# Two-head state blocks, paired w loads, u by matmul and a new instruction order in a fused linear-attention and mixing kernel

## Chip, cores, metric

One core of a Trainium2 chip. The metric is the device time of one execution in microseconds (us). "Span" is the profile's time from the first to the last instruction of one execution, some 1.7 us shorter. Ratios below are the mean time of one kernel's fast runs over that of the kernel before's fast runs of the same rounds, with a 95% interval, so not quite the ratio of the medians. A run counts as slow when it is over 1.5% above the fastest of its kernel; slow runs are left out of every ratio.

## The reference

```python
# B, H, S, D = 4, 8, 768, 48; all float32
for t in range(S):                                    # one state of 48 x 48 per head
    cur = einsum('bhd,bhe->bhde', u * k[t], v[t])
    y[t] = einsum('bhd,bhde->bhe', r[t], state + cur)
    state = w[t][..., None] * state + einsum('bhd,bhe->bhde', k[t], v[t])
x = y as (B, S, H*D)                                  # d_model 384
theta = x @ w_theta
mix = w_tok_r @ (x * cos(theta)) + w_tok_i @ (x * sin(theta))
un = x + mix
out = un + relu(un @ w_ch)
```

## The kernel before

Tokens go in 24 chunks of 128 (6 for each of 4 batches). In a chunk the decays are summed as logarithms by matmuls with triangular masks, exponentials give `a`, and q = r·a, k' = k·a turn the recurrence into matmuls: masked scores (`p`), their product with v, and the state of the chunk before times q. Heads sit in pairs: two heads of 48 dimensions, each padded to 64, fill 128 partitions. `ORDER` is a searched list of all operations; each engine receives its own in that sequence, and a number after a slash picks another engine. A buffer takes a free slot of its pool when its first writer is issued; `bank` is a pool of six 2 KB PSUM banks.

```python
SLOTS = {"cum": 1, "bank": 6, ...}

ys = [Buf("bank", [L, NP, D], f32) for _ in range(2)]        # y: one bank for each head of a pair
...
# state times q: 8 matmuls on 64 rows
def f_ys():
    for j in range(NP):                                      # NP = 4 pairs
        for e in range(2):
            ro = e * DP                                      # DP = 64
            nc.tensor.matmul(get(ys[e])[:, j, :], lhsT=get(qkt)[ro:ro + DP, j, :],
                             rhs=get(prev)[ro:ro + DP, j, :], start=(j == 0), stop=False, ...)
...
m = Buf("bank", [L, NP, D], f32)
def f_M():                                                   # state update: 8 matmuls of 64 columns
    if c > 0:
        nc.tensor.matmul(mt, lhsT=ident, rhs=get(prev), start=True, stop=False, ...)
    for j in range(NP):
        for e in range(2):
            h = 2 * j + e
            nc.tensor.matmul(mt[e * DP:(e + 1) * DP, j, :], lhsT=get(kk)[:, h, :], rhs=get(vb)[:, h, :], ...)
def f_S():
    nc.vector.tensor_tensor(get(Sb), get(m), get(alt).to_broadcast([L, NP, D]), op=ALU.mult)
...
def f_x():                                                   # two instructions
    for e in range(2):
        nc.vector.tensor_tensor(xv[:, e], get(ys[e]), bv[:, e], op=ALU.add)
...
nc.sync.dma_start(out=get(bf), in_=src[b, :, c*L:(c+1)*L, :].rearrange("h t d -> t h d"))   # 1024 runs of 192 B
nc.sync.dma_start(out=u_bc, in_=u.partition_broadcast(L))                                   # u, 192 KB
```

Of the kernel before, what the change touches and what calls it, by code (L numbers as in the profile page):

```python
# [10 lines left out]
AF = mybir.ActivationFunctionType  # L11
ALU = mybir.AluOpType

ORDER = """
669 1 97 0 98 2 670 671 672/1 99 101/1 104/1 3 102/1 108 109 110 113 114 111 112 685 4 103 686 105 106 107 9 21 100
145 117 118 5 6 677 217 218 7 121 10 13 687 688 11 115 8 128/1 129/1 219 122 123 14 126/1 124 119 146 125 25 120 148
22 132 130 133 15 147 150 169 17 23 149/1 12 127 170 171 152/1 153 176 238 172 134 116 139 156 678 157/1 131 679 154
173/1 140 18 19 135/1 239 680/1 241 158 193 174 137 138 161/1 180 665 689 136/1 220/1 240 16 20 151 159 181 141 142
194 221 177/1 200/1 661 24 162/1 195 182 183 198 143 227 155 201/1 160 228/1 163 165 144 197/1 185/1 186/1 666 204 673
28 690 667 691 668 202 175 199 178 205 206 166 681 26 223 224 164 187 179 692/1 209/1 207 167 229 232/1 184 210/1 188  # L20
230 208 211 189 196 27 33 213 30 168 203 662/1 713 190 721 214 233/1 714 715 222 191 225 212 29 192/1 31 226 37 722
231 717 693 215 242 674/1 245 716 34 723 234 235 725 675 663 236 32 35 216 724 718 243 237/1 269 729 719 682/1 720 726
727 730 246 676/1 41 733 734 731 244 683 809 701 818 735 684/1 249 732 728 270 262 736 250 247 810 251 252 263 264 267
265 819 286 271 827 820 293 287 821 694 253 811 266/1 822 254 39 812 695 813 36 289 696/1 38 288 310 273 828 290 248
274 664 275 829 276 277 697 42 311 313 278 268 279 43 256 255 258 40 257 830 831/1 291 272 259 823 814 824 280 297 294
312 45 282 705 44 334 298/1 335 281 49 702 815 283 709 337 295 336 46 832 260 284 299 315 47 292 296 703 261/1 53 57
302 48 54 836 285/1 737 704/1 314 833 300 304 741 738 317 341 305 834 339 301 55 51 739 303 698/1 306 50 307 321 742
743 52 338/1 322/1 699 308 309/1 700 837 318 323 740 342 745 324 59 325 845 345 838 316 328 839 58 746 846 56 747 358
326 327 319 329 840 61 340 346 347 350/1 359 360 706/1 343 379 320 344 330 351/1 361 847 62 841 707 331 65 848 364 332
849 63 842 352 843 708 365 380 333 382 850 710/1 711 348 851/1 66 712 349 67 354 353 403 381 427 362/1 69 749 355 816  # L30
368 854 70 60 369 825 370 73 748 371/1 372/1 64 363 404 356 357 405 366 367 373 374 855 375 753 744 406 68 407 852/1
410 856 857 863 376 377 82 428 386 408/1 414 411 750 384/1 754 378/1 751 757 858/1 383/1 434 752 415 755 71 758 387
759 76 756 430 872 390 760 416 881 429 75 385 412 432 873 409 419 397 864 435/1 451 431/1 420 452 398 413 391 392
417/1 418/1 865 85 882 388 438 874 454 395/1 453 396/1 423 393 394 475 883 424 826 421 389 399 422 476 482 456 859 884
455 72 439/1 478 400 477 890 83 866 458/1 885 499 860 480 861 80 867 440 441/1 875 500 459/1 442/1 462 74 401 436 90
81 433 483/1 463 876 402/1 425 426/1 443 444 891 501 479 892 520 445 464 886 437 502 77 465/1 457 460 887/1 486 521
466/1 461 447 446 469 467/1 523 487 893 448 488 862 468/1 899 522 491/1 470 489 503 492/1 449 505 450/1 471 481 765
490 894 509 78 472 835 473 484 766 510 877 474 895 878 495 896/1 767 504 761 485 762 900 79 879 511 496 763 888/1
525/1 506 527 512/1 497 498/1 769 513/1 764 773 493 777 901 897/1 770 771 526 768 778 524 494 779 908 87 853 909 507
508 538 902 772 575 528/1 529 926 774 775 544 868 539 903/1 514 515 530 592 91 545 516 910 93 911 869/1 551 568 517  # L40
531 576 780 904 547 518 546 623 95 935 519/1 624 870/1 532/1 548/1 781 549/1 782 917 912/1 555 86 599 569 776 783 784
905/1 533 571 570 936 918 577 89 906/1 534 625 572 552/1 556 913 536/1 889 550 88 914/1 593 616 562 640 927 537/1 594
915/1 573/1 595 557 597 937 560/1 919 944 535 553 920 928 596/1 921 561/1 938 554 598 558 92 579 617 540 618 945 580
541 542 871 563 559 581 84 939/1 543/1 564 946 916 603 953 565 620 604/1 584 619 94 585 566 929 922 582 641 954 621
583 574 567 923 642 930/1 605 588 600 627 601 924 955 578 907 586 608/1 606 589 628 607 789 790 956 587 590 591/1 940
791 880 629 957 644 643 785 941 793 602 630 817 786 787 609/1 632/1 646/1 633/1 647 931 650 96 932/1 792 612 794 613
651 795 796 622 933/1 648 626 962 958 788 942 614 844 652 655/1 631 610 963 656/1 611 615/1 959/1 645 636 637 960/1
971 653 634 649 635 947 948/1 898 654 638 797 925 943 657 639 964 798 949 801 799 961 658 659 660/1 1011 805 802 803
804 800 1001 972 806 965 807 981 1002 808 1003 966/1 967 973 974 1012 1013 950 951 1004 982 991 975 1014 968 1005 992
1006/1 1007 1015 993 983 1016 976/1 977 1008/1 1009/1 934 984 1021 1010 969 1022 1023 970 985 978/1 952 994 979/1 995  # L50
1017 980 1024 1025 1018 986 987 988 1019 989 1020 996 990 997 1026 1027 998 999 1000 1028 1029 1030
# [63 lines left out]
def kernel(  # L115
# [13 lines left out]
    nc = tc.nc  # L129
# [11 lines left out]
    MERGE = False  # L141
    HHW = set()
# [4 lines left out]
             "xT": 9, "sc": 3, "wf": 3, "wn": 3, "un": 4, "uT": 3, "o": 8}  # L147
# [12 lines left out]
    u_bc = cpool.tile([L, H, D], f32, name="u_bc")  # L160
    hpi = cpool.tile([L, 1], f32, name="hpi")
# [9 lines left out]
            for n in ("lw", "q", "k")}  # L171

# [15 lines left out]
    nc.vector.memset(hpi, HALF_PI)  # L188
    for n_ in ("lw", "q", "k"):
        for t_ in pads[n_]:  # L190
            nc.vector.memset(t_[:, :, D:], 0.0)
    make_upper_triangular(nc, mask_exc[:, 0, :], val=1.0, diag=False)
# [73 lines left out]
    def attention(n):  # L266
# [17 lines left out]
        ys = [Buf("bank", [L, NP, D], f32) for _ in range(2)]  # L284
# [50 lines left out]
        P.op("cuml" if last else "cum", f"cum{n}", [("PE", f_cum)], [lw], [cum])  # L335
# [90 lines left out]
        def f_ys():  # L426
            for j in range(NP):
                for e in range(2):
                    ro = e * DP
                    nc.tensor.matmul(get(ys[e])[:, j, :], lhsT=get(qkt)[ro:ro + DP, j, :],  # L430
                                     rhs=get(prev)[ro:ro + DP, j, :],
                                     start=(j == 0), stop=False, skip_group_check=True)

        def f_pS():
            f_p()
            f_ys()
        if MERGE and prev:
            P.op("pS", f"p{n}", [("PE", f_pS)], [qkt] + pr_, ph + ys)
        else:
            P.op("p", f"p{n}", [("PE", f_p)], [qkt], ph)  # L440
# [14 lines left out]
        if not last:  # L455
            m = Buf("bank", [L, NP, D], f32)
            Sb = s["S"] = Buf("S", [L, NP, D], bf16)

            def f_M():
                mt = get(m)  # L460
                if c > 0:
                    nc.tensor.matmul(mt, lhsT=ident, rhs=get(prev), start=True, stop=False,  # L462
                                     skip_group_check=True)
                for j in range(NP):
                    for e in range(2):
                        h = 2 * j + e
                        nc.tensor.matmul(mt[e * DP:(e + 1) * DP, j, :], lhsT=get(kk)[:, h, :],  # L467
                                         rhs=get(vb)[:, h, :], start=(c == 0 and j == 0), stop=True,
                                         skip_group_check=True)
            P.op("M" if c > 0 else "M0", f"M{n}", [("PE", f_M)], [kk, vb] + ([prev] if prev else []), [m])  # L470

            def f_S():
                nc.vector.tensor_tensor(get(Sb), get(m), get(alt).to_broadcast([L, NP, D]), op=ALU.mult)
            P.op("S", f"S{n}", [("DVE", f_S)], [m, alt], [Sb])

        def f_y():
            if prev and not MERGE:
                f_ys()
            for e in range(2):
                for j in range(NP):  # L480
                    nc.tensor.matmul(get(ys[e])[:, j, :], lhsT=get(p)[:, e, j, :],  # L481
                                     rhs=get(vb)[:, 2 * j + e, :],
                                     start=(c == 0 and j == 0), stop=True, skip_group_check=True)
# [168 lines left out]
```

## Time and profile before

| | before |
|---|---|
| median (lowest to highest, 3 runs) | 172.62 us (171.29 to 172.9) |
| span of the profiled run, clock | 168.7 us, 0.996 |
| busy: TensorE, VectorE, ScalarE, GpSimd | 142.2, 137.8, 118.6, 116.3 us |
| DMA packets, MB | 105990, 29.98 |

No engine is full over the whole span; the limits change from stage to stage, so the prediction reads busy time by stage. The lines for that stand in it. A group's line gives busy us and the mean ns of one instruction; the chain's pieces are start, length, what.

### The profile page before, as it was taken

The numbers are of one execution on the slowest core, as the hardware profiler recorded it, in microseconds if no ns is written. First come the engines' busy times: TensorE is split into PE (matmuls) and PEld (weight loads), VectorE is DVE, ScalarE is ACT, GpSimd is POOL, SyncE is SP. The second block draws the span as 40 slices with busy tenths as digits, with TensorE's granted clock in tenths as the row PEclk, the third lists the DMA queues.
The fourth block names the chain that finished last, engine by engine and source line by source line (L and its number), as shares of the span: only waits on it lengthen the run. The fifth ranks groups of instructions, "written<-read, shape, count | busy, mean of one in ns | idle before, by whom it ended". The sixth has DMA issues, their size and how long they took to land. (4 is left out here: it accounts for less than half of the span.)

```text
span 168.7 us, 4451 instructions
## 1 busy us (share of the span) xinstructions
PE 142.2 (84%) x1688; PEld 93.5 (55%) x1688; DVE 137.8 (82%) x284; ACT 118.6 (70%) x224; POOL 116.3 (69%) x126
## 2 busy tenths in 40 slices
PE   0437789488869999999876999999889999999990
PEld 0324466464446766676544767556556766666660
DVE  2364479999999999989999998699999898753462
ACT  3454788989558799999873889899976588460240
POOL 3021588987925959796996999999998876800030
PEclk9999999999999999999999999999999999999998
DMA  5999999999989999898999898995335711100055
GB/s 142 278 206 254 205 184 236 286 299 193 247 231 229 241 195 269 162 216 174 205 198 193 177 232 176 233 186 137 79 93 155 222 47 49 61 36 4 0 187 190
DMA packets 105990, 29.98 MB, mean 178 GB/s; under 512 B 100464, under 2 KB 104432, under 8 KB 105968
## 3 DMA queue, kind: packets, MB, share of 16 engines
q1 hardware_dynamic: 105968, 29.70, 78.7%
q8 instruction: 13, 0.21, 0.5%
q14 instruction: 9, 0.07, 0.2%
HBM read 24.97 MB, written 4.72 MB: 176 GB/s over the span
## 5 line engine op out<-in xcount | busy, mean ns | idle before, releaser
L545 PE MATMUL bank<-z_all,wtokT 128*128 128x384 bf16 x288 | 53.6, 326 | 1.8 <-DVE z_all L531 1.7
L545 PEld LDWEIGHTS <-wtokT 128*128 128x128 bf16 x288 | 26.5, 98 | 17.7 <-issue 2.4
L399 POOL TENSOR_TENSOR bon<-v,rub 128x384 bf16<-128x384 bf16 x24 | 21.9, 914 | 8.0 <-ACT v L351 3.8
L357 POOL TENSOR_TENSOR ruk<-ru,ink 128x384 bf16<-128x384 f32 x16 | 17.9, 1126 | 7.8 <-DVE ru L357 7.5
L330 ACT ACTIVATE a<-cum 128x768 f32<-128x768 f32 x24 | 19.5, 812 | 4.6 <-PE cum L326 3.0
L531 DVE TENSOR_TENSOR z_all<-x_all,sc 128x768 bf16<-128x768 bf16 x24 | 21.1, 894 | 1.2 <-ACT sc L525 1.2
L357 POOL TENSOR_TENSOR ru<-inr,u_bc 128x384 f32<-128x384 f32 x18 | 21.0, 1170 | 0.2
L343 POOL TENSOR_TENSOR k<-ink,a 128x384 bf16<-128x384 f32 x16 | 17.2, 1075 | 5.0 <-ACT alt L333 3.4
L444 DVE TENSOR_TENSOR p<-bank,mask_exc 128x512 bf16<-128x512 f32 x29 | 19.5, 681 | 1.0 <-PE bank L421 0.8
L579 POOL TENSOR_TENSOR o<-o,un 128x384 f32<-128x384 f32 x10 | 10.4, 1044 | 13.3 <-ACT o L576 13.3
L343 POOL TENSOR_TENSOR q<-inr,a 128x384 bf16<-128x384 f32 x13 | 14.9, 1147 | 5.7 <-ACT alt L333 3.8
L450 POOL TENSOR_SCALAR_AFFINE_SELECT p<-p 128x512 bf16<-128x512 bf16 x19 | 14.8, 780 | 4.9 <-ACT p L447 4.9
L493 DVE TENSOR_TENSOR x_all<-bank,bon 128x192 bf16<-128x192 f32 x48 | 14.7, 349 | 3.8 <-PE bank L481 2.3
L551 DVE TENSOR_TENSOR un<-bank,x_all 128x384 bf16<-128x384 f32 x24 | 12.8, 549 | 5.6 <-PE bank L545 3.0
L226 ACT ACT_TABLE_LOAD x12 | 15.4, 1283 | 1.0 <-PEq L636 0.8
L517 PE MATMUL bank<-wth,xT 128*128 128x384 bf16 x72 | 15.2, 327 | 0.8 <-DVE xT L506 0.6
L447 ACT ACTIVATE p<-bank 128x512 bf16<-128x512 f32 x19 | 11.3, 596 | 5.5 <-PE bank L421 4.9
L322 PE MATMUL cum<-lw,mask_exc 128*128 128x384 bf16 x24 | 8.9, 372 | 7.3 <-ACT lw L318 5.4
L522 ACT ACTIVATE sc<-bank 128x384 bf16<-128x384 f32 x24 | 11.8, 495 | 4.7 <-PE bank L517 2.5
L568 PE MATMUL bank<-wch,uT 128*128 128x384 bf16 x72 | 15.0, 325 | 0.0
L318 ACT ACTIVATE lw<-inw 128x384 bf16<-128x384 f32 x24 | 12.4, 525 | 3.6 <-DMA inw<-in_w_dram 3.6
L560 ACT ACTIVATE uT<-bank 128x384 bf16<-128x384 bf16 x14 | 6.6, 489 | 10.9 <-PE bank L556 10.8
(64 smaller groups left out, 309.1 us busy)
## 6 DMA issues: line engine op xcount, KB each, us to landing
inw<-in_w_dram SPq DMA_DIRECT2D x24, 192.0 KB, 4.3
inr<-in_r_dram SPq DMA_DIRECT2D x24, 192.0 KB, 4.3
ink<-in_k_dram SPq DMA_DIRECT2D x24, 192.0 KB, 4.2
inv<-in_v_dram SPq DMA_DIRECT2D x24, 192.0 KB, 4.2
out_dram<-o SPq DMA_DIRECT2D x24, 192.0 KB, 2.3
wf<-in_moe_w_tok_i_dram SPq DMA_DIRECT2D x6, 384.0 KB, 4.3
wf<-in_moe_w_tok_r_dram SPq DMA_DIRECT2D x6, 384.0 KB, 4.7
wf<-in_moe_w_theta_dram SPq DMA_DIRECT2D x1, 576.0 KB, 6.8
```

The costliest lines, as they stand in the source:

```text
L226: nc.scalar.preload_act_table_set("trig_and_small" if mode == "S" else "natural_log_exp_and_others")
L330: nc.scalar.activation(get(a), get(cum)[:, :, :DM], AF.Exp)
L343: eng.tensor_tensor(get(o)[:, :, :D], get(x), av, op=ALU.mult)
L357: eng.tensor_tensor(o_, get(x), y if y is u_bc else get(y), op=ALU.mult)
L399: nc.gpsimd.tensor_tensor(get(bon), get(vb), get(rub).to_broadcast([L, H, D]), op=ALU.mult)
L444: nc.vector.tensor_tensor(get(p)[:, e], get(ph[e]), mask_exc.to_broadcast([L, NP, L]), op=ALU.mult)
L450: nc.gpsimd.affine_select(out=get(p)[:, e], in_=get(p)[:, e], compare_op=ALU.is_gt, fill=0.0, base=0, pattern=[[0, NP], [1, L]], channel_m ...
L493: nc.vector.tensor_tensor(xv[:, e], get(ys[e]), bv[:, e], op=ALU.add)
L517: nc.tensor.matmul(get(th), lhsT=get(s["xT"])[:, j, :], rhs=wth[:, j, :], start=(j == 0), stop=(j == NJ - 1))
L531: nc.vector.tensor_tensor(z_all[:, b, c], xb, get(sc), op=ALU.mult)
L545: nc.tensor.matmul(get(ac), lhsT=wtokT[:, q_, s_, ti, :], rhs=z_all[:, b, s_, q_, :], start=(s_ == 0 and q_ == 0), stop=(s_ == NCH - 1 and ...
L568: nc.tensor.matmul(get(ml), lhsT=get(uT)[:, j, :], rhs=wch[:, j, :], start=(j == 0), stop=(j == NJ - 1))
```

## The change

Intent: fewer and wider matmuls for the state (four of 128 rows and 96 columns in place of eight half-size ones), which takes a state padded with zeros off the diagonal of each pair; y then needs one bank instead of two; larger packets for w in chunks 1 to 8 (two neighbouring tokens are contiguous, 384 B); and no 192 KB broadcast of u. The order was searched anew.

```diff
-    HHW = set()
+    HHW = set(range(1,9))            # chunks whose w comes in token pairs (code already there:
+                                     # two loads of 64 partitions, 8+4 small matmuls for the sums)
-        ys = [Buf("bank", [L, NP, D], f32) for _ in range(2)]
+        ys = Buf("bank", [L, H, D], f32)
-            m = Buf("bank", [L, NP, D], f32)
+            m = Buf("bank", [L, NP, 2, D], f32)          # state tiles: zeroed once, [L, NP, 2, D]
                 for j in range(NP):
-                    for e in range(2):
-                        nc.tensor.matmul(mt[e*DP:(e+1)*DP, j, :], lhsT=get(kk)[:, h, :], rhs=get(vb)[:, h, :], ...)
+                    nc.tensor.matmul(mt[:, j], lhsT=get(kk)[:, 2*j:2*j+2, :], rhs=get(vb)[:, 2*j:2*j+2, :], ...)
             def f_S():
-                nc.vector.tensor_tensor(get(Sb), get(m), get(alt).to_broadcast([L, NP, D]), op=ALU.mult)
+                for e in range(2):
+                    rows = slice(e * DP, (e + 1) * DP)
+                    nc.vector.tensor_tensor(get(Sb)[rows, :, e, :], get(m)[rows, :, e, :],
+                                            get(alt)[rows].to_broadcast([DP, NP, D]), op=ALU.mult)
-            (state times q: eight matmuls on rows ro:ro+64)
+                for j in range(NP):
+                    nc.tensor.matmul(y[:, 2*j:2*j+2, :], lhsT=get(qkt)[:, j, :], rhs=get(prev)[:, j], ...)
-            for e in range(2):
-                nc.vector.tensor_tensor(xv[:, e], get(ys[e]), bv[:, e], op=ALU.add)
+            nc.vector.tensor_tensor(x_all[:, b, c, :]..., get(ys), get(bon), op=ALU.add)
-    u_bc <- u.partition_broadcast(L)                                 (DMA)
+    u_row <- u (1.5 KB DMA); u_ps = one_row.T @ u_row (TensorE); u_bc = copy of u_ps (ScalarE)
-ORDER = (old list)
+ORDER = (new list)
```

## The prediction

> **What bounds the kernel now.** I read the busy shares by slice first, then busy time by stage, then the chain that ended last, then the groups by shape. The slices, each 4.2 us wide:
>
> ```profile
> PE   0437789488869999999876999999889999999990
> DVE  2364479999999999989999998699999898753462
> DMA  5999999999989999898999898995335711100055
> ```
>
> The DMA engines are full from the start to about slice 27 (114 us), VectorE is full from slice 6 to 30, TensorE from slice 26 to the end. Three stages, three limits. Busy time by stage (columns: stretch and length, then busy us and instructions of PE, PEld, DVE, ACT, POOL, then clock, DMA share, GB/s):
>
> ```profile
> 0.00:24.00 24.00, 11.88 (x111) 8.22 (x112) 10.90 (x33) 12.84 (x24) 8.09 (x17) 1.00 1.04 216
> 24.00:100.00 76.00, 66.66 (x874) 44.28 (x872) 73.98 (x141) 62.20 (x117) 63.14 (x63) 1.00 1.03 220
> 100.00:150.00 50.00, 48.83 (x604) 32.00 (x603) 44.47 (x95) 39.91 (x76) 43.27 (x46) 1.00 0.53 129
> 150.00:168.70 18.70, 14.81 (x105) 8.98 (x103) 8.46 (x18) 3.69 (x8) 1.79 (x2) 0.96 0.24 86
> ```
>
> Until 24 us VectorE idles 13.1 us while DMA runs at a share of 1.04: loads set the pace. From 24 to 100 us VectorE is busy 74.0 of 76 us, with DMA still at 1.03. From 100 us on TensorE is busy 48.8 of 50. The DMA share of the small loads is a matter of packets, as the DMA view of 14 to 26 us shows:
>
> ```profile
> DMA packets 12768, 2.43 MB, mean 202 GB/s; under 512 B 12767, under 2 KB 12767, under 8 KB 12767
> q1 hardware_dynamic: 12767, 2.41, 106.9%
> ```
>
> 12 us x 16 engines x 1.069 / 12767 = 16.1 ns for a packet of 192 bytes, so 1024 of them (one 192 KB load) cost 1.0 us. The chain is, after 100 us, nearly all TensorE in queue order, and its pieces are start-to-start times (start, us, what):
>
> ```profile
> 102.46 0.33 PE bank L421 x8
> 102.79 1.08 PE bank L545 x6
> 103.87 0.17 PE bank L499 x3
> 104.04 0.20 PE bank L430 x8
> 104.24 0.31 PE bank L481 x8
> ...
> 136.49 0.08 PE bank L462
> 136.57 0.24 PE bank L467 x8
> 136.81 0.59 PE bank L517 x3
> ...
> 139.64 0.49 PE bank L568 x3
> ```
>
> Six 384-column matmuls take 0.97 us elsewhere in this chain and 1.08 after L421; three take 0.49 and, after L467, 0.59. So leaving a row- or column-tiled group (L421 scores, L430 state times q, L467 state update) costs some 0.10 us. The groups that I price with (busy us, mean ns):
>
> ```profile
> L473 DVE TENSOR_TENSOR S<-bank,alt 128x192 bf16<-128x192 f32 x20 | 6.9, 347 | 0.1
> L493 DVE TENSOR_TENSOR x_all<-bank,bon 128x192 bf16<-128x192 f32 x48 | 14.7, 349 | 3.8 <-PE bank L481 2.3 <-POOL bon L399 1.2
> L551 DVE TENSOR_TENSOR un<-bank,x_all 128x384 bf16<-128x384 f32 x24 | 12.8, 549 | 5.6 <-PE bank L545 3.0 <-POOL o L579 2.6
> ```
>
> **What the Trainium skill says.** (1) "TensorEngine Tiling (Array Packing)", Key Properties: changing the tiling mode drains TensorE. The trace agrees, with 0.10 us per change. (2) "TensorE: Matmul & The Clock Gate", under "Wait — 56ns, not 53.3ns?": starts never lie closer than about 25 ns. L430's eight 48-column matmuls take 0.20 us, 25 ns each, and not the 20 ns of their columns; four 96-column ones (estimate 40 ns each from 163 ns per 384) are therefore cheaper than eight. (3) "DMA: Bandwidth & Descriptors", Specifications: below 512 B a transfer is not at line rate. The 16.1 ns per 192 B above agree; what 384 B cost no run shows yet. (4) "SBUF — State Buffer", Who interferes with whom: a VectorE instruction with two SBUF inputs contends with a GpSimd one that reads SBUF. z (L531), same shape each time, lasts 541 to 1365 ns here, median 850.
>
> **The change part by part.**
>
> *State update.* Eight 48-column matmuls into two column tiles become four 96-column ones, and the identity matmul that carries the state goes from 192 to 384 columns. Before: 0.08 + 0.24 + 0.10 for leaving the mode = 0.42 us. After: 0.16 + 4 x 0.04 = 0.32. Gain 0.10 us.
>
> *State times q.* Before 0.20 + 0.30 (the L481 matmuls behind it, which take 0.22 where no tiled group precedes) = 0.50. After 0.16 + 0.22 = 0.38. Gain 0.12. Over about 20 chunks both make 4.4 us of TensorE, of which half (chunks 12 on) lies in the TensorE-bound part.
>
> *VectorE.* The state is now scaled by two instructions on 64 partitions instead of one on 128: the same length per partition, so +0.27 us start to start, 20 times, +5.4 us. The sum x becomes one 384-column instruction (0.46 start to start, as for un) in place of two (0.53): -1.7 us. The new order moves more: masking on VectorE 29 to 40 (+11 x 0.60), final relu+add 14 to 23 (+9 x 0.46), against q 11 to 3 (-8 x 0.83), copies of the transposed q,k 17 to 10 (-7 x 0.60), casts 6 to 2. Summing all instructions ahead of the last x by the mean durations gives 141.7 us before, 139.1 after: VectorE is not relieved by much. ScalarE goes from 119 to 121, GpSimd from 118 to 112 by the same sum. The mix is kinder to the shared port, since eight two-SBUF-input products leave VectorE.
>
> *w in token pairs, chunks 1 to 8.* 512 packets of 384 B instead of 1024 of 192 B; estimate 0.65 us for a load instead of 1.0, so -2.6 us of DMA over eight. The price is 12 small matmuls for the running sums instead of 6: estimate +0.1 us each on TensorE, in a stage where it has room, and 10 small GpSimd instructions at the start (2.7 us, hidden behind the first load).
>
> *u.* A 192 KB broadcast load becomes 1.5 KB, one matmul and one ScalarE copy (0.49 us): -0.6 us of DMA at the very start.
>
> *Order.* Reading the two orders against each other and pricing loads at 1.0 (small), 0.65 (paired) and 1.3 us (384 KB of weights), the load of v for chunk 11 ends its queue at 69.6 us before (it was issued at 67.8 to 69.5 us, so the sum is sound) and at 65.5 after: -4.1. k of chunk 4 stands behind 25.8 us of loads before, 12.0 after, as weights move back. So VectorE's 13.1 idle us at the start should shrink.
>
> **The sum**, in profile time, cut where z of chunk 11 ends (86.7 us) and where the last angle matmul (chunk 23) ends (150.4 us). *First part:* loads -4.1, VectorE idle perhaps -3, VectorE work about -1; the engines are in lockstep, so I credit 2.5. *Second part:* TensorE bound, 61.7 us of queue before and 58.3 after (y -1.2, state update -0.9 and one fewer of them, three final matmul groups deferred -1.5, one transposition more +0.5); 3.4 less, of which I credit 2.5, as VectorE is 89% busy there. *Last part:* 14.3 us of TensorE before (60 + 21 wide matmuls, 7 transposes), 15.2 after (60 + 27, 6): +0.9. Total -4.1 of 168.7, so 164.6; times 172.62/168.7 gives 168.4. I take **168.3 us**.
>
> **Rivals.**
>
> *A, VectorE takes it all back.* Scaling the state adds 5.4 us to the engine that is full from 24 to 100 us, and it sits on the recurrence from chunk to chunk. For it: 74.0 busy of 76. Against: the same order takes as much off VectorE elsewhere, and L473 idles it only 0.1 us. It would leave 171 to 173 us.
>
> *B, loads are hidden.* The waits show only 3.6 us of ScalarE and 2.3 us for inputs, so shorter loads would not matter after 24 us; then the first part gives 1 us or less and the time is 170. For it: VectorE full from 24 us. Against: the 13.1 us idle before that, and the early k loads.
>
> *C, more than I credit.* The sum x needs one bank instead of two of the six, so scores and transposes can start earlier, and the order was searched with that freedom. If the idle of the start falls by 4 us and TensorE's whole 3.4 us comes through, the time is 165 us.
>
> *D, the searched order does not carry over.* A tight order that depends on modelled durations meets real contention: 541 to 1365 ns for one shape. A few waits of 1 to 2 us each would eat the gain: 172 us.
>
> **Range and chances.** B and C bracket the sum, A and D are the upper end; C with a better start makes the lower. I put 164.5 to 172.0 for 8 in 10. The 2% line is 169.2, little above my centre, and the before runs alone spread over 171.29 to 172.9. Chances: faster 0.60, same 0.36, slower 0.04.
>
> **What would show it.** Right: VectorE idle in the first 24 us at 10 us or less; matmul groups behind the state update and state-times-q without the extra 0.10 us, and those groups at 0.32 and 0.16 us; paired w loads near 0.65 us of DMA; z of chunk 11 ending near 84 us, the last angle matmul near 145.5, and some 15 us of TensorE after it. Wrong: the two half scalings of the state costing over 0.60 us together, VectorE full past 145 us, a TensorE gap over 1 us after 90 us, or DMA as long per load with 384 B packets.

## The result, and the profile after

| | before | after |
|---|---|---|
| median (lowest to highest, 4 runs each) | 172.76 us (171.29 to 173.13) | 167.82 us (167.45 to 171.75) |
| ratio of fast runs | | 0.9723 (0.965 to 0.9795) |
| span, clock of the profiled run | 168.7 us, 0.996 | 166.0 us, 0.988 |
| busy: TensorE, VectorE, ScalarE, GpSimd | 142.2, 137.8, 118.6, 116.3 | 143.7, 135.8, 122.4, 109.1 |

Faster by 2.8%, 0.5 us from the predicted time. The profiled execution of the kernel before took 170.48 us, less than any of its timed runs in the table, that of the changed kernel 167.72, in the middle of its own: so the profiles differ by 2.7 us where the medians differ by 4.9, and the account by stages below covers the 2.7 only. The stages of the changed kernel, in the columns of the prediction's table (the last row ends with the span):

```profile
0.00:24.00 24.00, 12.89 (x123) 8.48 (x124) 12.63 (x37) 12.90 (x25) 15.70 (x32) 1.00 0.95 176
24.00:100.00 76.00, 69.76 (x838) 49.07 (x839) 70.45 (x141) 68.35 (x121) 59.50 (x60) 0.98 1.02 221
100.00:150.00 50.00, 49.32 (x541) 33.21 (x539) 44.94 (x90) 39.37 (x74) 33.91 (x36) 1.00 0.59 139
150.00:166.00 16.00, 11.75 (x85) 7.09 (x82) 7.82 (x16) 1.81 (x4) 0.00 (x0) 0.98 0.32 113
```

From 24 to 100 us VectorE fell from 74.0 to 70.5 us busy and TensorE rose from 66.7 to 69.8: the middle stage is now balanced between the two. At the start VectorE still idles 24.0 - 12.6 = 11.4 us.

Where the 2.7 us of span came from shows when the profile is cut where the prediction cut it: at the end of z of chunk 11 and of the last angle matmul (TensorE busy us, instructions, clock, DMA share, GB/s; first the kernel before, then the changed one):

```profile
86.70:150.40 63.70, 60.49 (x756) 1.00 0.64 143
```

```profile
87.50:146.60 59.10, 58.42 (x676) 1.00 0.71 158
```

The first part did not get shorter (86.7 to 87.5 us), the second lost 4.6 us, the last grew from 18.3 to 19.4. A second trace of the changed kernel (after_again below, span 165.1) has 86.5, 59.3 and 19.3: the last two parts repeat, the first varies by 1 us from run to run. TensorE's instructions in order of time in the changed kernel (start, length, line, tile, shape, count) show the state groups:

```profile
66.74 0.33 PE L451 MATMUL bank<-S,ident 128*128 128x384 bf16 x1
66.90 0.33 PE L453 MATMUL bank<-v,k 128*128 128x96 bf16 x4
67.07 0.33 PE L325 MATMUL cum<-lw,mask_exc 128*128 128x384 bf16 x1
...
142.15 0.33 PE L468 MATMUL bank<-S,qkt 128*128 128x96 bf16 x4
142.32 0.36 PE L473 MATMUL bank<-v,p 128*128 128x48 bf16 x8
142.53 1.14 PE L530 MATMUL bank<-z_all,wtokT 128*128 128x384 bf16 x6
```

Start to start, the update takes 67.07 - 66.74 = 0.33 us (predicted 0.32) and state times q 0.17 (predicted 0.16), the product behind it 0.21; nothing is lost in front of or behind them. That part of the prediction is right to 0.01 us.

VectorE pays more than predicted. Its instructions in the changed kernel, and then in the kernel before:

```profile
101.93 0.71 DVE L460 TENSOR_TENSOR S<-bank,alt 64x192 bf16<-64x192 f32 x2
102.68 0.56 DVE L478 TENSOR_TENSOR x_all<-bank,bon 128x384 bf16<-128x384 f32 x1
```

```profile
111.32 0.34 DVE L473 TENSOR_TENSOR S<-bank,alt 128x192 bf16<-128x192 f32 x1
111.58 0.54 DVE L365 TENSOR_REDUCE rub<-ruk 128x8 f32<-128x384 bf16 x1
```

The two half scalings hold VectorE 0.75 us start to start, the one before 0.26. Predicted was 0.54. What came to VectorE's help is z, of the same shape and count in both kernels (groups by shape, busy us and mean ns; before, then after):

```profile
L531 DVE TENSOR_TENSOR z_all<-x_all,sc 128x768 bf16<-128x768 bf16 x24 | 21.1, 894 | 1.2 <-ACT sc L525 1.2
```

```profile
L516 DVE TENSOR_TENSOR z_all<-x_all,sc 128x768 bf16<-128x768 bf16 x24 | 16.6, 694 | 1.4 <-ACT sc L510 1.3
```

4.5 us less for the same work. Most of it comes with the order: the same line is at 20.3 us with the state's part alone under the old order (old_state below) and at 18.3 with the new order alone (oldcode_neworder). That GpSimd, with 7 us less to do, stands less often in its way is what the Trainium skill's page "SBUF — State Buffer", Who interferes with whom, would say of two SBUF inputs beside a GpSimd read; here it is an inference from the durations, no run isolates it, and GpSimd's total alone does not rank the kernels (105.6 us busy in oldcode_neworder, 109.1 in the changed one).

The DMA did not get cheaper either. The queue's packets, MB and share of 16 engines' span, before and after:

```profile
q1 hardware_dynamic: 105968, 29.70, 78.7%
```

```profile
q1 hardware_dynamic: 101858, 29.50, 80.8%
```

0.787 x 168.7 x 16 = 2124 us of engine time before, 0.808 x 166.0 x 16 = 2146 after, for 4110 packets fewer. In the packet records of the trace a 384 B packet took 29.7 ns on average (median 22), a 192 B one 16.1 before and 16.5 after (median 15): a paired load costs 512 x 29.7 / 16 = 0.95 us, not the estimated 0.65. The Trainium skill ("DMA: Bandwidth & Descriptors", Specifications) puts the size for line rate at 512 B and more; 384 B took on average 8 to 10% less per byte than 192 B, so a paired load saved some 0.1 us.

### The profile page after: what moved, and what is told of

It is laid out like the page before. It is cut to its first block, busy times and chain, and to the rows that moved or that the text cites.

```text
span 166.0 us, 4230 instructions
## 1 busy us (share of the span) xinstructions
PE 143.7 (87%) x1578; PEld 97.8 (59%) x1578; DVE 135.8 (82%) x282; ACT 122.4 (74%) x222; POOL 109.1 (66%) x126
## 4 chain that ended last, share of the span: by engine, by line
PE 43%; DVE 26%; POOL 10%; issue 8%; DMA 3%; ACT 1%; SPq 0%; POOLq 0%; DVEq 0%
PE bank L530 21%; PE bank L553 5%; DVE p L433 5%; POOL q L346 3%; PE bank L502 3%; DVE S L460 3%; DVE x_all L478 3%; DVE z_all L516 3%; PE bank L409 3%; DMA ink<-in_k_dram 3%; DVE o L558 2%; PE bank L424 2%; POOL bon L402 2%; DVE rub L368 2%; PE bank L541 2%
## 5 line engine op out<-in xcount | busy, mean ns | idle before, releaser
L346 POOL TENSOR_TENSOR q<-inr,a 128x384 bf16<-128x384 f32 x21 | 23.3, 1108 | 9.8 <-ACT alt L336 4.5
L433 DVE TENSOR_TENSOR p<-bank,mask_exc 128x512 bf16<-128x512 f32 x40 | 26.6, 682 | 1.8 <-PE bank L424 1.4
L416 ACT ACTIVATE qkt<-bank 128x1024 bf16<-128x1024 bf16 x14 | 14.2, 1026 | 5.0 <-PE bank L409 5.0
L516 DVE TENSOR_TENSOR z_all<-x_all,sc 128x768 bf16<-128x768 bf16 x24 | 16.6, 694 | 1.4 <-ACT sc L510 1.3
L502 PE MATMUL bank<-wth,xT 128*128 128x384 bf16 x72 | 16.1, 339 | 0.1
L558 DVE SCALAR_TENSOR_TENSOR o<-bank,un 128x384 f32<-128x384 f32 x23 | 12.4, 551 | 3.8 <-PE bank L553 3.5
L460 DVE TENSOR_TENSOR S<-bank,alt 64x192 bf16<-64x192 f32 x40 | 14.0, 351 | 1.7 <-PE bank L453 1.4
L333 ACT ACTIVATE a<-cum 128x768 f32<-128x768 f32 x16 | 13.1, 820 | 2.2 <-PE cum L329 1.4
L510 ACT ACTIVATE sc<-bank,hpi 128x384 bf16<-128x384 f32 x24 | 13.9, 589 | 0.0
L354 ACT ACTIVATE v<-inv 128x384 bf16<-128x384 f32 x24 | 12.7, 535 | 1.4 <-DMA inv<-in_v_dram 1.4
L478 DVE TENSOR_TENSOR x_all<-bank,bon 128x384 bf16<-128x384 f32 x24 | 13.1, 550 | 0.3
```

Source lines behind the costliest of these rows:

```text
L346: eng.tensor_tensor(get(o)[:, :, :D], get(x), av, op=ALU.mult)
L433: nc.vector.tensor_tensor(get(p)[:, e], get(ph[e]), mask_exc.to_broadcast([L, NP, L]), op=ALU.mult)
L460: nc.vector.tensor_tensor(get(Sb)[rows, :, e, :], get(m)[rows, :, e, :], get(alt)[rows].to_broadcast([DP, NP, D]), op=ALU.mult)
L478: nc.vector.tensor_tensor(x_all[:, b, c, :].rearrange("p (h d) -> p h d", h=H), get(ys), get(bon), op=ALU.add)
L502: nc.tensor.matmul(get(th), lhsT=get(s["xT"])[:, j, :], rhs=wth[:, j, :], start=(j == 0), stop=(j == NJ - 1))
L516: nc.vector.tensor_tensor(z_all[:, b, c], xb, get(sc), op=ALU.mult)
```

## The experiments

Twelve runs, on two chips, each beside runs of the kernel before in the same rounds: old_state, old_pairs, old_all and after_again in one series on the first chip; oldcode_neworder, new_nopairs, new_Mhalf and new_S1 in a second, and nopairs_S1, new_splitload, new_ubcast and new_S2full in a third, both on the other. The changed kernel itself was not run in the last two. There its 0.9723 and 0.9689 are ratios from other rounds, with intervals of 0.965 to 0.9795 and 0.9619 to 0.976, and a kernel whose interval overlaps them is told from it by midpoints only.

### The parts under the old order

**old_state**: the kernel before with the state's part of the diff above and nothing else.

> The kernel before, its old order, with the state alone changed (padded two-head blocks, full-width matmuls, y in one bank, two half scalings). In the trace of the changed kernel two half scalings take 0.74 us start to start where one took 0.27, so VectorE gets +0.47 x 20 = 9.4 us, less 0.07 x 24 = 1.7 for the sum x; TensorE loses some 4.4 us. Theory (the state is a trade of TensorE time for VectorE time, and pays only with an order that fits): ratio to before 1.00 to 1.02. Rival (full width pays by itself): 0.985 or less.

Measured: 177.07 us, ratio 1.0213 (1.0163 to 1.0263). VectorE was busy 147.1 us, 9.3 more than before.

**old_pairs**: the kernel before with

```diff
-    HHW = set()
+    HHW = set(range(1, 9))
```

> The kernel before with w of chunks 1 to 8 in token pairs and nothing else. Theory: a 384 B packet took 29.7 ns on average in the changed kernel against 16.1 for 192 B, so a paired load saves under 0.1 us of DMA and the ratio to before is 0.995 to 1.005. Rival (as predicted, 0.35 us saved a load at the start): 0.985.

Measured: 174.45 us, ratio 1.0073 (1.0036 to 1.011): slower, just past the expected 1.005.

**old_all**: all code of the change, and the old order with the indices shifted for the two added operations of u.

> All code of the change (state, pairs, u by matmul) under the old order, the three u operations put where the one load stood. Theory (the gain is the new order's, on the bank that the one-bank y frees): ratio to before 0.995 to 1.02. Rival (the parts carry their gain with them): 0.985 or less.

Measured: 180.0 us, ratio 1.0392 (1.0347 to 1.0436). Worse than either theory said. The state (2.1 points) and the pairs (0.7) alone explain 2.8 of the 3.9; whether the rest is u by matmul or the parts together, no run shows.

**after_again**: the changed kernel unaltered.

> The changed kernel unaltered, on the same chip as the three partial ones: ratio to before 0.965 to 0.98 as measured. It is the other end of the comparison with all parts under the old order.

Measured: ratio 0.9689 (0.9619 to 0.976), from the two fast runs of six (166.86 and 168.7 us; the median over all six is 169.97).

So the code of the change alone makes the kernel 3.9% slower, and going from the old order to the new with that code is worth 0.9689/1.0392 = 0.932. The theory that the parts carry their gain with them fails. This does not show yet that the order does it alone.

### The order without the parts

**oldcode_neworder**: the kernel before under the new order. It does not fit as it stands: at eleven places the order asks for a bank while y holds two. Each such operation is put off to the first place where a bank is free.

```diff
-ORDER = (old list)
+ORDER = (new list without the two operations of u; M15, M20, ml11, ml21, p6, th12,
+         tqk16, xt13, y14, y15, y18 deferred)
```

> The kernel before, all its code, in the new order. Eleven operations find no free bank there because y takes two, and each is put off to the first place where one is free (M15, M20, ml11, ml21, p6, th12, tqk16, xt13, y14, y15, y18); nothing else moves. Theory A (the order is the gain, and the state in full width is only a trade of 4.4 us of TensorE against 7.7 of VectorE): ratio to before 0.965 to 0.985, as the changed kernel. Theory B (order and one-bank y need each other): 0.995 or more, with TensorE waiting behind the deferred operations.

Measured: 170.34 us, ratio 0.9817 (0.9749 to 0.9885), theory A's range. The order alone gives 1.8% (the eleven operations moved by a few places). But theory A also held that the state would be a mere trade. It is not, under this order: the next run is this kernel with the state in blocks and u by matmul added, in the same rounds.

**new_nopairs**: the changed kernel with

```diff
-    HHW = set(range(1,9))
+    HHW = set()
```

> The changed kernel with every w loaded plainly, running sums as in the rest. The kernel before got 0.7% slower with pairs alone. Theory (384 B packets save too little and the small matmuls cost TensorE): ratio to before 0.960 to 0.972, no slower than the changed kernel's 0.969 to 0.972. Rival (in this order, which starts with five w loads, pairs pay as predicted): 0.985.

Measured: 165.54 us, ratio 0.9553 (0.9501 to 0.9604). Faster than the changed kernel and beyond the theory's own range. Two things follow.

First, state and u together are worth 0.9553/0.9817 = 0.973 under the new order, while the state alone cost 2.1% under the old. The 24 to 100 us rows of the two kernels of the trade, state without new order (old_state) and new order without state (oldcode_neworder), suggest why:

```profile
24.00:100.00 76.00, 63.55 (x725) 43.10 (x723) 73.30 (x129) 58.27 (x107) 57.41 (x58) 0.94 1.03 220
```

```profile
24.00:100.00 76.00, 71.38 (x918) 48.91 (x915) 69.29 (x144) 69.12 (x124) 59.12 (x61) 0.96 1.01 222
```

Under the old order VectorE is the full engine (73.3 of 76) and TensorE has 12 us to spare: a change that takes from TensorE and gives to VectorE loses. Under the new order, before the state changes, TensorE is the fuller (71.4 against 69.3), since q products and copies have left VectorE: there the same change wins. This is a reading of two rows and not an experiment: the rows lie at clocks of 0.94 and 0.96, and the same 1688 matmuls were busy for 142.2 us in the profile before, at a clock of 0.996, and for 144.1 in oldcode_neworder, at 0.980; so the lead of 2.1 us is not sharp. In the TensorE-bound second part, from z of chunk 11 to the last angle matmul, oldcode_neworder takes 86.4 to 148.3 = 61.9 us against 59.1 in the changed kernel and 63.7 before: of the 4.6 us gained there the order alone brings 1.8. Some of the other 2.8 us may belong to the eleven deferred operations; no run separates the two.

Second, the pairs cost 1.4 to 1.7% by midpoints (the intervals of the changed kernel begin at 0.9619 and 0.965, that of new_nopairs ends at 0.9604). The start shows where. SyncE issues the loads (start, length, what, count); the changed kernel, then the one without pairs:

```profile
0.80 1.39 SPq L244 DMA_DIRECT2D inw<-in_w_dram  x2
2.24 0.60 SPq L249 DMA_DIRECT2D inw<-in_w_dram  x1
2.88 1.25 SPq L244 DMA_DIRECT2D inw<-in_w_dram  x2
4.17 0.60 SPq L249 DMA_DIRECT2D inr<-in_r_dram  x1
4.82 1.25 SPq L244 DMA_DIRECT2D inw<-in_w_dram  x2
6.12 0.51 SPq L574 DMA_DIRECT2D urow<-in_u_dram  x1
6.68 1.01 SPq L249 DMA_DIRECT2D ink<-in_k_dram  x2
```

```profile
0.80 2.01 SPq L249 DMA_DIRECT2D inw<-in_w_dram  x3
2.86 0.71 SPq L249 DMA_DIRECT2D inr<-in_r_dram  x1
3.60 1.05 SPq L249 DMA_DIRECT2D inw<-in_w_dram  x1
4.70 0.48 SPq L574 DMA_DIRECT2D urow<-in_u_dram  x1
5.23 1.13 SPq L249 DMA_DIRECT2D ink<-in_k_dram  x2
```

A load of half the partitions holds SyncE as long as a whole one, some 0.6 us, so a paired w takes 1.25 us of issue and the k loads go out 1.45 us later. Meanwhile the DMA engines wait for work: from 2 to 8 us their mean share is 0.80 in the changed kernel and 1.05 without pairs. VectorE's first product starts when k lands; that line in the changed kernel, then without pairs:

```profile
10.98 0.92 DVE L346 TENSOR_TENSOR k<-ink,a 128x384 bf16<-128x384 f32 x1 [8.13 <-DMA ink<-in_k_dram]
```

```profile
10.12 0.91 DVE L346 TENSOR_TENSOR k<-ink,a 128x384 bf16<-128x384 f32 x1 [7.59 <-DMA ink<-in_k_dram]
```

By the first copy of a transposed weight VectorE is 1.65 us ahead without pairs (22.57 against 24.22 us), and z of chunk 11 ends at 85.7 us instead of 87.5. So a part of the first part's lost gain is here: the second trace of the changed kernel has the same late start (k at 11.16, the weight copy at 24.36), but z of chunk 11 at 86.5, so between 0.8 and 1.8 us of it remain by then.

**new_splitload**: is it the second issue, or the six extra matmuls and the packets? Plain w, plain sums, two issues.

```diff
+        def fn_s():                                  # w of chunks 1 to 8, plain layout
+            for g in range(2):
+                rows = slice(g * DP, (g + 1) * DP)
+                nc.sync.dma_start(out=get(bf)[rows], in_=src[b, :, c*L + g*DP : c*L + (g+1)*DP, :]
+                                  .rearrange("h t d -> t h d"))
```

> The kernel without pairs, but w of chunks 1 to 8 loaded plainly by two issues of 64 partitions each: packets of 192 B and the plain running sums, only the second issue is back. Theory (the cost of the pairs is the second issue: SyncE takes some 0.6 us for each while the first loads go out, and the first k lands at 10.98 us instead of 10.12): ratio to before 0.966 to 0.974. Rival (it is the six extra small matmuls per chunk or the 384 B packets): 0.953 to 0.958, as without pairs.

Measured: 168.0 us, ratio 0.9642 (0.9571 to 0.9713). The midpoint lies 0.9 points over new_nopairs, below the theory's range, and the intervals overlap. Its start is the changed kernel's: first k at 11.17 us, the weight copy at 24.43 (its profile is of a slow run, but two fast ones of the changed kernel show the same). So the second issue explains the late start. That it is worth 0.9 of the 1.4 to 1.7 points is a matter of midpoints; the interval reaches into the rival's range, and the rest (packets, extra matmuls) is not separated from noise.

**new_ubcast**: the u part of the diff undone in the changed kernel.

> The changed kernel with u loaded as one 192 KB broadcast again, no matmul and no copy for it. As predicted, the matmul form saves 0.6 us of DMA at the very start: 0.972 to 0.976. Rival (the queue is bound by issues there and not by bytes, and the two matmul passes of u took 1.6 us of TensorE time at 8 us): no change or a gain, 0.964 to 0.971.

Measured: ratio 0.980 (0.9755 to 0.9846), from seven fast runs of 22 (167.58 to 169.76 us). Undoing it costs some 0.9 points by midpoints, more than the 0.3 expected, though the intervals overlap with the changed kernel's; the rival's range lies outside. The first k product starts at 12.19 us instead of 10.98 (11.16 in the second trace; the 12.19 is from a slow run): the 192 KB lie in the queue ahead of k, and delay it by 1.0 to 1.2 us, about twice the 0.6 us estimated. If u is worth the same without pairs, some 1.8 of the 2.7 points above are left for the state; no run has the state alone in the new order.

### The state's own terms

**new_Mhalf**: the state update alone back to half width.

```diff
-                    nc.tensor.matmul(mt[:, j], lhsT=get(kk)[:, 2*j:2*j+2, :], rhs=get(vb)[:, 2*j:2*j+2, :], ...)
+                    for e in range(2):
+                        h = 2 * j + e
+                        nc.tensor.matmul(mt[e*DP:(e+1)*DP, j, e, :], lhsT=get(kk)[:, h, :], rhs=get(vb)[:, h, :], ...)
```

> The changed kernel with the state update again in eight half-width matmuls into two column tiles; the state stays padded. TensorE gets 0.16 + 0.24 + 0.10 for leaving the mode = 0.50 us per chunk against 0.33 measured, +0.17 x 20 = 3.4 us, about half of it after chunk 11. Theory (TensorE bounds that part): +1 to 2 us, ratio to before 0.975 to 0.985. Rival (TensorE has room): as the changed kernel, 0.969 to 0.972.

Measured: 169.87 us, ratio 0.9814 (0.9762 to 0.9865), 0.9 to 1.3 points over the changed kernel by midpoints (clear of one of its two intervals, overlapping the other), some 1.6 to 2.2 us for 3.4 us of TensorE time. In its trace the update takes 0.25 + 0.24 us, against 0.33: the 0.09 us around the tiled group are back. Where the time is lost does not follow the theory: the second part takes 59.2 us (90.4 to 149.6), as in the changed kernel, and the first ends 3 to 4 us later, but its middle stage ran at a clock of 0.93 there. The trace does not separate the two.

**new_S1**: one scaling instruction with a decay that carries the zeros.

```diff
-        alt = Buf("alt", [L, NP], f32)               # decay of the chunk
+        alt tiles [L, NP, 2], zeroed once; two exponentials write alt[rows of head e, :, e]
-                for e in range(2): (half scaling, 64 partitions)
+                nc.vector.tensor_tensor(get(Sb), get(m), get(alt).to_broadcast([L, NP, 2, D]), op=ALU.mult)
```

> The changed kernel with the state scaled by one VectorE instruction of 128 x 384: the decay is kept twice per pair of heads with zeros on the off-diagonal half (two small ScalarE exponentials instead of one, some +0.06 us each start to start), so the zeros come from the product. VectorE 0.46 us instead of 0.74, 20 times: -5.6 us. Theory (VectorE still sets the pace from 24 to 100 us): -1.5 to -3 us, ratio to before 0.955 to 0.962. Rival (VectorE has slack now, 5.5 us idle there): 0.969 to 0.972.

Measured: ratio 0.9636 (0.958 to 0.9691), between theory and rival; the midpoint is 0.5 to 0.9 points under the changed kernel, within the intervals. The instruction takes 0.46 us start to start, as worked out, so 20 x 0.29 = 5.8 us of VectorE time bought about 1 us. That VectorE no longer decides does not follow, because it did not get 5.8 us less to do: z took 19.4 us in this trace, a slow run, and 19.2 in nopairs_S1, a fast one, against 16.6, and VectorE's busy time fell only from 135.8 to 134.3 us. ScalarE got 4.9 us more.

**new_S2full**: as new_S1, but two instructions of 128 partitions x 192.

> The changed kernel with the state scaled by two instructions of 128 partitions x 192 instead of two of 64 x 192, with the zero-padded decay. For the duration alone: two halves took 0.74 us start to start. If it is two short instructions as such that cannot overlap on one tile, again 0.72 to 0.76; if it is the 64 partitions, 0.53 to 0.56, as the two instructions of x in the kernel before.

Measured (VectorE in order of time):

```profile
64.20 0.61 DVE L464 TENSOR_TENSOR S<-bank,alt 128x192 bf16<-128x192 f32 x2
64.73 0.55 DVE L562 SCALAR_TENSOR_TENSOR o<-bank,un 128x384 f32<-128x384 f32 x1
```

0.53 us start to start for the pair, against 0.75 for the two on 64 partitions with the same 192 elements each. Each instruction by itself takes the same 0.35 us; the halves do not overlap each other or what follows by the 0.08 us that full ones do. The run changes two things, the 64 partitions and the start at partition 64, and the changed kernel's trace points to the start: the first half, at partition 0, begins 0.08 us before its predecessor ends, as any other (18 of 20 times); the second begins 0.01 us after the first has ended, and the next instruction, back at partition 0, 0.03 us after the second. A memset of a single partition at the start of the trace overlaps its successor by 0.04 us, so few partitions alone do not prevent it. No run moves the start alone.

### Both findings together

**nopairs_S1**: new_nopairs with new_S1's scaling.

> The changed kernel with both findings: w loaded plainly and the state scaled by one VectorE instruction with a zero-padded decay. Alone they gave 0.955 and 0.964 against the changed kernel's 0.969 to 0.972. If they act on different stages (start and VectorE-bound middle) they add: 0.946 to 0.951. If both only shorten the same wait: 0.955.

Measured: 165.3 us, ratio 0.9512 (0.9451 to 0.9574), fast runs 163.68 to 165.32 us. The best ratio of all, 4.9% under the kernel before and 1.8 to 2.1 points under the changed one, but not apart from new_nopairs (0.9553) by the intervals. The sum of both is near the middle between "they add" and "they do not".

## Why the prediction was right

The time (168.3 for 167.82) and the class were right. Step by step:

- **State update and state times q, 0.10 and 0.12 us a chunk**: right to 0.01 us in the trace, and new_Mhalf costs time when the update's part is undone, by midpoints 0.9 to 1.3 points; that it does so in the TensorE-bound part is not shown.
- **Second part, 3.4 us less by count, 2.5 credited**: it gave 4.6. The stage is TensorE-bound as said (58.4 busy of 59.1 us). I gave a discount for a VectorE at 89%; instead the 2.0 us of gaps left in that stage before (63.7 less 61.7 by the same count) shrank as well, to 0.8 (59.1 less 58.3). The signs named for it came true: no TensorE gap of 1 us after 90 us, and VectorE not full past 145 us (2.1 busy of 5 from 145 to 150).
- **First part, -2.5 us**: failed, it was +0.8 (-0.2 in the second trace). Two terms of the sum were mis-sized. The load term took 0.65 us for a paired load and -4.1 us up to v of chunk 11; it was 0.95 us of packets and two issues of 0.6 us where DMA was not yet the limit, and the issue of v of chunk 11 ended at 71.1 us (70.7 in the second trace) and not at 65.5: 1.6 later than before. new_nopairs has it at 69.4 and ends this part at 85.7 us, 0.8 to 1.8 earlier. And the idle of VectorE, "10 us or less", was 11.4 (10.0 without pairs). Pricing each load by its packets missed that the first loads are bound by how fast SyncE can issue them. (The eight paired loads of the prediction, at 0.35 us each, are 2.8 us and not 2.6.)
- **Scaling the state, +0.27 us**: +0.49 in its place (0.75 against 0.26), so +10 us of VectorE and not 5.4. By my own criterion (over 0.60 us together) this step was wrong. That it did not show in the time is put down here to z, 4.5 us cheaper, and to the copies and products that the order took off VectorE; this is argued and not shown. new_S1 gives back only some 1 us of it, but z takes half of what it saves.
- **u, -0.6 us**: right in sign; new_ubcast makes it 1.0 to 1.2 us at the first k and, by midpoints, some 0.9% of the time.
- **Last part, +0.9 us**: 18.3 to 19.4, right.
- **Rival A** (VectorE takes it back) is what happens under the old order: +2.1%, 9.3 us more VectorE time. The prediction dismissed it by the sum of work, and not by which engine is full under the order in question, which by the runs seems to decide. **Rival B** had the right size for the first part for the wrong reason. **Rival C** was right that the freed bank matters to the order: the new one finds no bank at eleven places without it; how much of the time hangs on that is open. **Rival D** (the searched order does not carry over) did not come true: the order alone gave 1.8%.

So the total is the sum of two errors of opposite sign, -2.1 us more than credited in the second part and +3.3 in the first, and should not be read as proof of the working. By the profile it is off by 1.4 us (166.0 for 164.6); that the time came within 0.5 is luck too, since the factor 172.62/168.7 carried over a profile of the kernel before that was faster than its timed runs. In ratios: the order alone 0.982, state and u 0.973 on top, pairs 1.016 to that (0.9706, the mean of the changed kernel's two results, over 0.9553); the product is 0.971 by construction. How much a search on the old code would have found with its two-bank y stays open; no such order was made.

## What to carry to other kernels

A change that moves time from one engine to another need not have a value of its own: read which engine is full in the stage under the order it will run in, and test code and order apart, since here the code alone was 3.9% slower and code with order 2.8% faster. While a queue is still empty, count DMA issues and not bytes: splitting a load in two for bigger packets doubled the issue time, and delayed the first dependent work by 0.9 us. When a tuned kernel changes in several parts at once, undo each alone; one of them may be losing (dropping the pairs gave another 1.4 to 1.7%).

## What the Trainium skill lacked or had wrong

- "DMA: Bandwidth & Descriptors", Issuing engines are not separate DMA queues: it calls the sequencer's time to initiate a DMA usually small relative to the DMA. Here SyncE took 0.60 us to issue a 192 KB load and as long for 96 KB, against about 1.0 us of transfer; with two issues per w the start was bound by it.
- The same page, Specifications: it gives 512 B as the size for line rate, but no measured time of a packet just below. 384 B packets took 29.7 ns on average (median 22) against 16.1 to 16.5 (median 15) for 192 B, a gain of 8 to 10% per byte on average.
- "TensorEngine Tiling (Array Packing)", Key Properties: it says that a mode change drains TensorE, without a size. Here a tiled group costs 0.09 to 0.10 us for it.
- "VectorE: DVE Perf Modes", Two Vector instructions with no wait between them: it gives a model of which instructions start only when the earlier ones have finished (where the start partition changes), but not what it costs. Here two of 64 x 192 from PSUM, at partitions 0 and 64, took 0.75 us start to start, two of 128 x 192 at partition 0 took 0.53.
